# Two of eight weight loads split into one 96-row part and four 8-row parts, in an attention and swish feed-forward kernel

## The chip, the core and the metric

The kernel runs on one core of a Trainium2 chip. The metric is device time in microseconds for one execution. A profiled execution has a span, from its first to its last instruction, which is a little shorter than the device time.

The names in the text: PE does matrix products (its weight loads, PEld, run beside them), ACT applies functions and copies, DVE and POOL do elementwise work, and SP issues transfers, which are carried out by 16 DMA engines.

## The reference

Linear attention on 8 batches, 8 heads, 576 positions and a head size of 64, followed by a layer with a swish whose slope differs by channel:

```python
q_s = exp(q - max(q, -1));  q_s = q_s / sum(q_s, -1)      # softmax over the head dimension
k_s = exp(k - max(k, 2));   k_s = k_s / sum(k_s, 2)       # softmax over positions
kv  = einsum('bhsd,bhse->bhde', k_s, v)
x   = einsum('bhsd,bhde->bhse', q_s, kv)                  # then to [4608, 512]
h   = x @ w_in                                            # w_in: 512 x 2048
g   = h / (1 + exp(-beta * h))
out = g @ w_out                                           # w_out: 2048 x 512
```

Inputs and output are float32; the matrix products run in bf16.

## The kernel before

**Stages.** A chunk is 512 of a batch's 576 positions, with one batch per chunk (chunks 0 to 6 and 8); chunk 7 collects the 64 left-over positions of all eight batches. For each chunk, phase A computes 16 units of h (`unit_mm`, line 456, four matmuls of 128x512 each), a tanh on ACT (line 468) and g on DVE (line 470). Phase B (`b_mm`, line 508) multiplies g with w_out into `acc`, four tiles of 128 positions, 16 matmuls each. The matmuls of phase B are handed out in a fixed list `bq`, a few after each unit, so PE nearly always has one of the two kinds to run.

**The order is written out by hand** (`manual_schedule`, line 64): every engine runs its instructions in the order in which the program emits them.

**Start.** Batches 0 and 1 have a faster path of their own. The loads of batch 0, w_in (lines 557 to 563), beta and w_out (lines 564 and 565) are issued by SP one after the other at the program's start; those of batches 1 and 2 stand between and behind POOL's casts of w_out in the program (lines 637 to 650), but in SP's own queue they simply follow the w_out loads. Every load goes to a buffer of the pool `ld` (13 buffers), so a load also waits until the tile that had its buffer 13 loads earlier has been read.

**w_out.** The 16 slices of 128 rows come in eight loads wo0, wo2, ... wo14, each of 128 rows of 4 KB (two slices). POOL casts each to bf16 (`cast_w_out`, line 172, through the helper line 160) into `w_out_b`. The first user is phase B of chunk 0: its list takes slices 0 to 3 for the four tiles, then 4 to 7 for the four tiles, then 8 to 15 tile by tile.

**Batch 1** (`batch_1`, lines 653 to 705) follows phase A of chunk 0 in the program: 32 matmuls of phase B, then exponentials of q (`eq_exp`, line 193, ACT), their sums and divisions (`eq_sum` line 200, `eq_div` line 204, DVE), 6 and 14 more matmuls of phase B, transposes on PE (`eq_t`, line 216), exponentials of k (line 229), casts of v (line 160 on POOL, 151 on ACT, 165 on DVE), products of k and v (line 258), and x (`x_group`, line 407), with a few matmuls of phase B between them. Then phase A of chunk 1 starts.

**Completion.** In the built program, SP's transfers use eight semaphores in turn, and each transfer's issue waits until the one issued eight places before it has landed.

Of the kernel before, what the change touches and what calls it, by code (L numbers as in the profile page):

```python
# [16 lines left out]
def kernel(  # L17
# [10 lines left out]
    nc = tc.nc  # L28
    P = nc.NUM_PARTITIONS
# [38 lines left out]
    w_out_dram = moe_w_out.rearrange("(b p i) f -> b p i f", p=P, i=4)  # L68
# [23 lines left out]
    def unit(name):  # L92
        return ldp.tile([P, U], F32, tag="ld", name=name)
# [46 lines left out]

    def load_w_out(j0):
        t = unit(f"wo{j0}")[:, 0 : 2 * DM].rearrange("p (j n) -> p j n", j=2)
        nc.sync.dma_start(t, w_out_dram[j0 // 4, :, j0 % 4 : j0 % 4 + 2, :])
        ld["wo", j0] = t


# [417 lines left out]
    for j0 in range(0, NJ, 2):  # L564
        load_w_out(j0)
# [63 lines left out]
    for blk in range(1, 4):  # L629
        for k0 in (0, 2):  # L630
            if (blk, k0) == (1, 2):
                t, _ = ld["wi", 1, 2]
# [167 lines left out]
```

## Time and profile before

| What | Value |
|---|---|
| device time, three runs | 283.83, 283.87, 283.99 us (median 283.87) |
| the profiled execution | 283.87 us |
| its span | 282.1 us |
| PE busy | 274.6 us (97%), granted clock 1.0 |
| PEld, DVE, ACT, POOL busy | 135.7, 156.0, 168.4, 70.6 us |
| moved by DMA | 51.69 MB |
| w_out loads: number, size, issue to landing | 8, 512 KB, 10.3 us (median) |
| their issues by SP | 15.8 to 24.9 us from the span's start |
| POOL's casts of w_out | 8 of 1.04 us, starting at 26.1 to 35.2 us |

A reader of the profile should keep in mind that PE's busy time is counted with modelled ends, since matmuls overlap: a matmul of 128x512 counts for 379 ns but the next one starts 216 ns later. An average over the span says little here: the first 50 us have another limit than the rest, so the stages are read from timelines and windows.

The page's row of DMA activity, in 40 slices of 7.05 us, each digit the busy share in tenths, shows the same division:

```profile
DMA  7999999879699808990799059905100201031122
```

### The profile page before, as it was taken

How to read it: one execution, taken by the hardware profiler on the slowest of the kernel's cores; microseconds unless marked ns; L12 is line 12 of the kernel's file. 1: busy time of each engine (PE TensorE's matmuls, PEld its weight loads, DVE VectorE, ACT ScalarE, POOL GpSimd, SP SyncE). 2: the span in 40 equal slices, each digit the busy share in tenths (PEclk: the TensorE clock that was granted, in tenths of full speed). 3: DMA queues.
4: the chain of work that ended last, by engine and by line, in shares of the span. 5: the costliest groups of instructions: out<-in, count | busy, mean ns of one | idle time of the engine just before them, and what ended most of it. 6: DMA issues, size and time to landing. Idle time of an engine off the chain costs nothing.

```text
span 282.1 us, 4627 instructions
## 1 busy us (share of the span) xinstructions
PE 274.6 (97%) x1688; PEld 135.7 (48%) x1688; DVE 156.0 (55%) x283; ACT 168.4 (60%) x280; POOL 70.6 (25%) x116
## 2 busy tenths in 40 slices
PE   7799999999999999999999999999999999999995
PEld 3445444445444445444544444444444444444444
DVE  2768369977865475549564766476453444443301
ACT  5766368867965587557855785478454544444411
POOL 1468721550721063104510361027000000000000
PEclk9999999999999999999999999999999999999999
DMA  7999999879699808990799059905100201031122
GB/s 228 380 374 406 391 384 359 311 172 352 149 234 357 175 37 190 366 210 37 154 329 285 24 132 303 307 0 128 60 37 2 76 37 39 0 76 37 37 77 74
DMA packets 52054, 51.69 MB, mean 183 GB/s; under 512 B 21568, under 2 KB 42432, under 8 KB 52032
## 3 DMA queue, kind: packets, MB, share of 16 engines
q1 hardware_dynamic: 51888, 51.33, 60.0%
q8 instruction: 13, 0.21, 0.3%
q10 hardware_dynamic: 144, 0.07, 0.1%
q14 instruction: 9, 0.07, 0.1%
HBM read 38.28 MB, written 9.44 MB: 169 GB/s over the span
## 4 chain that ended last, share of the span: by engine, by line
PE 83%; DMA 12%; DVE 2%; ACT 0%; SPq 0%; issue 0%; ACTq 0%; POOL 0%
PE acc L508 40%; PE h L456 39%; DMA q<-in_q_dram 4%; DMA wo<-in_moe_w_out_dram 4%; DMA wi<-in_moe_w_in_dram 3%; DMA k<-in_k_dram 2%; PE kv L383 2%; PE x L407 2%; DVE Eq L204 1%; DVE qz L200 1%; ACT Eq L193 0%; SPq L116 0%; PE xt L421 0%; DVE qT L165 0%; PE kv L258 0%
## 5 line engine op out<-in xcount | busy, mean ns | idle before, releaser
L470 DVE SCALAR_TENSOR_TENSOR g<-th,h 128x512 bf16<-128x512 bf16 x144 | 97.3, 685 | 95.3 <-ACT th L468 95.0
L468 ACT ACTIVATE th<-h,beta_h 128x512 bf16<-128x512 f32 x144 | 97.2, 689 | 84.9 <-PE h L456 82.9
L508 PE MATMUL acc<-w_out_b,g 128*128 128x512 bf16 (+2 forms) x608 | 145.5, 368 | 0.0
L456 PE MATMUL h<-xT,w_in_b 128*128 128x512 bf16 x512 | 128.2, 379 | 0.0
L456 PEld LDWEIGHTS <-w_in_b 128*128 128x128 bf16 x576 | 65.0, 113 | 61.0 <-issue 0.5
L508 PEld LDWEIGHTS <-g 128*128 128x128 bf16 x608 | 56.8, 98 | 63.8 <-issue 2.5
L314 POOL TENSOR_TENSOR Eq<-Eq,qz 128x512 bf16<-128x512 bf16 x24 | 25.1, 1051 | 84.2 <-issue 41.0
L160 POOL TENSOR_SCALAR_AFFINE_SELECT va<-v 128x256 bf16<-128x256 f32 (+3 forms) x55 | 22.7, 450 | 13.8 <-DMA v<-in_v_dram 13.6
L537 ACT ACTIVATE o<-acc 128x512 f32<-128x512 f32 x34 | 20.0, 591 | 8.9 <-PE acc L508 8.9
L354 ACT ACTIVATE Ek<-k 128x640 bf16<-128x640 f32 x24 | 17.7, 736 | 0.0
L456 PE MATMUL h<-xTt,w_in_b 128*128 128x512 bf16 x64 | 16.4, 379 | 0.0
L312 DVE TENSOR_REDUCE qz<-Eq 128x8 f32<-128x512 bf16 x24 | 16.2, 676 | 0.0
L304 ACT ACTIVATE Eq<-q 128x512 bf16<-128x512 f32 x24 | 14.7, 622 | 0.0
L200 DVE TENSOR_REDUCE qz<-Eq 128x16 f32<-128x1024 bf16 x4 | 4.9, 1214 | 10.4 <-ACT Eq L193 10.4
L165 DVE CAST xT<-x 128x512 bf16<-128x512 f32 x15 | 10.3, 684 | 0.6 <-PE x L407 0.6
L581 PE MATMUL warm<-zf 128*128 128x512 f32 (+1 forms) x14 | 8.8, 772 | 1.5 <-DVE zf L548 1.5
L151 ACT CAST xT<-x 128x512 bf16<-128x512 f32 x17 | 9.7, 578 | 0.6 <-PE x L407 0.5
L160 POOL TENSOR_SCALAR_AFFINE_SELECT w_in_b<-wi 128x512 bf16<-128x512 f32 x15 | 9.2, 633 | 3.3 <-DMA wi<-in_moe_w_in_dram 3.1
L193 ACT ACTIVATE Eq<-q 128x1024 bf16<-128x1024 f32 x4 | 4.2, 1057 | 9.0 <-DMA q<-in_q_dram 9.0
L340 POOL TENSOR_TENSOR Et<-Et,zt 128x512 bf16<-128x512 bf16 x4 | 4.2, 1042 | 20.9 <-DVE zt L339 15.6
L160 POOL TENSOR_SCALAR_AFFINE_SELECT w_out_b<-wo 128x1024 bf16<-128x1024 f32 x8 | 8.3, 1042 | 1.8 <-DMA wo<-in_moe_w_out_dram 1.7
L407 PE MATMUL x<-qT,kvn 64*64 64x512 bf16 x64 | 5.8, 391 | 0.8 <-ACT xT L151 0.6
(48 smaller groups left out, 76.5 us busy)
## 6 DMA issues: line engine op xcount, KB each, us to landing
q<-in_q_dram SPq DMA_DIRECT2D x16, 512.0 KB, 6.0
out_dram<-o SPq DMA_DIRECT2D x31, 256.0 KB, 3.1
k<-in_k_dram SPq DMA_DIRECT2D x24, 320.0 KB, 6.6
v<-in_v_dram SPq DMA_DIRECT2D x24, 320.0 KB, 7.3
wo<-in_moe_w_out_dram SPq DMA_DIRECT2D x8, 512.0 KB, 10.3
wi<-in_moe_w_in_dram SPq DMA_DIRECT2D x6, 512.0 KB, 8.0
k<-in_k_dram SPq DMA_DIRECT2D x4, 576.0 KB, 9.1
v<-in_v_dram SPq DMA_DIRECT2D x6, 288.0 KB, 8.9
```

The lines of the kernel that those rows point to most:

```text
L160: nc.gpsimd.affine_select(out=dst, in_=src, pattern=[[0, n]], base=0, channel_multiplier=0, compare_op=ALU.is_equal, fill=fill0,)
L165: eng.tensor_copy(dst, src)
L304: nc.scalar.activation(by_pair(Eq[b], m).rearrange("p t h d -> p h t d"), ld["q", b, hf][:, a : a + 2, :].rearrange("p h (t d) -> p h t d" ...
L312: nc.vector.tensor_reduce(z, e, axis=AX.X, op=ALU.add)
L314: nc.gpsimd.tensor_tensor(e, e, z.unsqueeze(3).to_broadcast((P, NT, 2, D)), ALU.mult)
L354: nc.scalar.activation(Ek[b][:, :, h0:h1, :].rearrange("p t h d -> p h t d"), ld["k", b, hf][:, a : a + h1 - h0, :].rearrange("p h (t d) - ...
L407: nc.tensor.matmul(xps[b, 2 * g + c][o, :], kvn[b][r, j, :], qT[b][r, g, a] if b < EARLY else qT[b][r, :, j, :], start=True, stop=True,)
L456: nc.tensor.matmul(hs[n, i][:], w_in_b[:, kt, blk * CH + r : (blk + 1) * CH : 4], rhs_a(n, kt), start=(kt == 0), stop=(kt == KT - 1),)
L468: nc.scalar.activation(th[:], h[:], ACTF.Tanh, scale=beta_h[:, i // 4, i % 4 : i % 4 + 1])
L470: nc.vector.scalar_tensor_tensor(out=g[:], in0=th[:], scalar=1.0, in1=h[:], op0=ALU.add, op1=ALU.mult)
L508: nc.tensor.matmul(acc[n, st][:, c0:c1], gs[n, j][:, min(st, 3) * P : (min(st, 3) + 1) * P], w_out_b[:, j, c0:c1], start=(j == 0), stop=(j ...
L537: nc.scalar.activation(o[:], acc[n, st][:], ACTF.Copy, scale=0.5)
```

## The change

Two of the eight w_out loads, wo4 and wo10, are no longer one transfer of 128 rows. Their first 96 rows are one transfer; the other 32 rows are four transfers of 8 rows each, which are meant to run as one row on each of the first eight DMA engines. All five are issued by SP, one after the other, at the place of the old load. The tile, the bytes and the rest of the program stay the same; SP has 8 transfers more. The beta load behind w_in's second block stands in both kernels.

```diff
     def load_w_out(j0):
         t = unit(f"wo{j0}")[:, 0 : 2 * DM].rearrange("p (j n) -> p j n", j=2)
-        nc.sync.dma_start(t, w_out_dram[j0 // 4, :, j0 % 4 : j0 % 4 + 2, :])
+        src = w_out_dram[j0 // 4, :, j0 % 4 : j0 % 4 + 2, :]
+        if j0 in (4, 10):
+
+            nc.sync.dma_start(t[0:96], src[0:96])
+            for r in range(96, P, 8):
+                nc.sync.dma_start(t[r : r + 8], src[r : r + 8])
+        else:
+            nc.sync.dma_start(t, src)
         ld["wo", j0] = t
```

## The prediction

> **What bounds the kernel now.** I read the page's chain of waits first, then the timelines of the engines around its DMA part, then a table of windows. In the chain, the listing of its longest pieces in order of time (start, duration, what) has only DMA until 36.63 us and hardly anything but PE later:
>
> ```profile
> 15.77 10.30 DMA wo<-in_moe_w_out_dram
> 26.15 10.46 DMA q<-in_q_dram
> 36.63 1.06 ACT Eq L193
> 37.72 1.23 DVE qz L200
> 39.26 1.22 DVE Eq L204
> 40.48 1.14 DVE qz L200
> 41.94 1.23 DVE Eq L204
> ```
>
> Read it downward: a w_out load, the first q load of batch 1 (q1_0), its exponential on ACT, and four steps of DVE with only reciprocals between them. The DMA engines are the bound of the first 50 us, and the point at which their lateness becomes PE's is batch 1. The windows (length, busy time of PE, PEld, DVE, ACT, POOL with instructions, granted clock, DMA share, GB/s) show it, and one late stage that I need below:
>
> ```profile
> 28.00:32.00 4.00, 4.00 (x20) 1.92 (x19) 2.61 (x5) 2.42 (x4) 3.28 (x4) 1.00 1.03 410
> 40.00:44.00 4.00, 3.90 (x46) 2.22 (x44) 3.89 (x9) 3.63 (x8) 1.70 (x3) 1.00 1.07 374
> 44.00:48.00 4.00, 3.85 (x37) 1.61 (x35) 3.44 (x9) 3.03 (x8) 0.46 (x2) 1.00 1.08 358
> ...
> 248.06:249.30 1.24, 1.24 (x7) 0.60 (x6) 0.69 (x1) 0.21 (x1) 0.00 (x0) 1.00 0.97 207
> ```
>
> DMA share is 1 or above while w_out comes in, at 410 GB/s. PE is covered (4.00 of 4.00) and loses only 0.10 + 0.15 us between 40 and 48. How little slack is left there is read from PE's timeline (start, duration):
>
> ```profile
> 29.48 11.39 PE L508 MATMUL acc<-w_out_b,g 128*128 128x512 bf16 x52
> 40.70 0.61 PE L216 MATMUL tp<-ident,Eq 128*128 128x128 bf16 x8
> ...
> 42.52 0.60 PE L508 MATMUL acc<-w_out_b,g 128*128 128x512 bf16 x2
> 43.22 0.62 PE L216 MATMUL tp<-ident,Eq 128*128 128x128 bf16 x8
> ```
>
> The first division (line 204) ends at 39.26 + 1.22 = 40.48 and PE's transposes of it begin at 40.70: 0.22 us of slack. The second ends at 41.94 + 1.23 = 43.17, and PE starts 0.05 us later: none. So what delays q1_0 by D beyond 0.2 us delays PE by D once both transposes are through, and PE has no hole afterwards in which to recover it.
>
> **How the loads flow.** POOL's casts of w_out (line 160) start as each load lands:
>
> ```profile
> 27.41 1.04 POOL L160 TENSOR_SCALAR_AFFINE_SELECT w_out_b<-wo 128x1024 bf16<-128x1024 f32 x1 [0.23 <-DMA wo<-in_moe_w_out_dram]
> 28.68 1.04 POOL L160 TENSOR_SCALAR_AFFINE_SELECT w_out_b<-wo 128x1024 bf16<-128x1024 f32 x1 [0.23 <-DMA wo<-in_moe_w_out_dram]
> 29.97 1.04 POOL L160 TENSOR_SCALAR_AFFINE_SELECT w_out_b<-wo 128x1024 bf16<-128x1024 f32 x1 [0.25 <-DMA wo<-in_moe_w_out_dram]
> ```
>
> A load of 512 KB per 1.28 us. With 128 rows on 16 engines that is 8 rows each, 0.16 us per 4 KB row. From issue to landing it takes 10.3 us, so some eight loads stand in the queue. The trace also keeps 16 completion marks for every transfer, without the engine's number: for q1_0 the first stands at 34.77, the ninth at 35.31, the last at 36.61. This spread of 1.84 us is almost the same for all w_out loads (28.14, 28.71, 29.91 for wo6): some engines run behind for the whole stage, and only the last one releases the consumer.
>
> **The change, part by part.**
>
> *Other engines.* The built programs have the same instructions in the same order on PE, DVE, ACT and POOL; SP gets 8 more issues (4 after wo4, 4 after wo10). POOL's casts of these two tiles wait for five transfers in place of one.
>
> *The 96-row part.* 6 rows per engine by 0.16 = 0.96 us in place of 1.28. If rows 0 to 95 don't spread as evenly as 128 it may cost the old 1.28. I take 0.96.
>
> *The single-row loads.* Eight rows on eight engines, four times per tile. Free running, each costs those engines 0.16 us. From the other side: the nearest row of a transfer that touches few partitions is the stage of 64-partition stores, where at a DMA share of 0.97 the rate is 207 GB/s, half of 410. In proportion to partitions, 8 of them would get 26 GB/s, and 32 KB would take 1.27 us. So 0.16 to 1.27 us each. The row has only one halving in it, and I take that: 0.32 us. Per tile the eight engines then spend 0.96 + 4 x 0.32 = 2.24 us in place of 1.28, +0.96; for two tiles +1.92. The bounds: 0.96 + 4 x 0.16 = 1.60, +0.32 per tile, +0.64 for both; and 1.28 + 4 x 1.27 = 6.36, +5.1 per tile, +10.2 for both. The eight other engines are spared 2 rows per tile, 0.64 us for both.
>
> [...]
>
> *Who is late.* Which eight engines are meant can't be seen in the marks. If the last engine is among them, the landing is late by the full +1.92. If the latest of them is only the second last (1.53 behind the first, where the last is 1.83), by 1.92 - 0.30 = 1.6. One of these two holds in 3 of 4 draws of 8 out of 16. I take 1.8.
>
> *SP.* In the built program every load waits for the one issued eight places before it. The small loads fill places, so q1_0, which waited for wo0 and issued at 26.15, now waits for wo8, landing at 31.19 before, and is issued 5 us later. Its first packets are wanted at about 33.3, the first mark of wo14 before it; the first load of the kernel was issued at 0.80 and its packets started at 1.93, so they can start at 31.2 + 1.1 = 32.3. Covered by 1.0 us. The four small loads of wo10 wait for wo4's parts (28.6), and SP's issues of loads take 0.33 to 0.85 us, so wo12 is issued at 30.3 to 32.3 in place of 23.51, and starts at 31.4 to 33.4; the last engine reaches it at 32.5. That is 0 to 0.9 us; I take 0, and keep 0.9 for the range. Behind these issues in SP's queue stand wo12, wo14, q1, k1, v1 and batch 2. As 8 issues were added, each load from q2 on waits for the same one as before.
>
> *w_out itself.* A late cast would stop PE only beyond its slack. wo10's cast ends at 33.57; PE takes its rows as matmuls 35 and 36 of the 52 that start at 29.48, at 36.9: 3.3 us. wo14's ends at 36.20 and is wanted at 37.8: 1.6 us. A lateness of 1.8 just reaches the latter (0.2 us), and this is part of the same 1.8, not beside it: the transposes wait for q1_0 anyway.
>
> **Sum.** 1.8 us on q1_0, less 0.22 at the first transposes, and the 0.22 returns at the second ones, where PE already waits: +1.8 us. The profiled execution took 283.87 us (282.1 of span and 1.8 around it), as the median of the runs does. 283.87 + 1.8 = 285.7.
>
> **The rivals.**
>
> *A, the eight engines lead.* Should these be the early ones and rows cost 0.16, then the late ones are spared 0.64 us and everything from q1_0 on lands 0.64 earlier. PE can use it: it idles 0.25 us by the windows, and by its starts the matmuls at 43.22, 44.63 and 44.96 come 0.26, 0.22 and 0.24 later than where PE doesn't wait, 0.72 in all. 283.87 - 0.64 = 283.2. For it: the spread exists, and 0.64 is near the gap between its halves (the second eight of the marks begin 0.57 after the first). Against it: the very last engine, 0.7 behind the next at wo6, must be spared too, and the rows must be free of the halving.
>
> *B, the eight engines hold the last one, and rows run freely.* +0.64: 284.5. For it: DMA share of 1 through the stage. Against: needs the few partitions to cost nothing.
>
> *C, it cancels.* Early engines take the extra within their 1.5 us of lead, the last one isn't touched, or is spared what SP's late issue takes back: 283.9. The point from which this gives way is a lateness of 0.2 us at q1_0.
>
> **How the numbers follow.** Forecast 0.55 (285.7; its own range 284.6 to 288), B 0.16 (284.5), A 0.16 (283.2), C 0.13 (283.9). About 0.2% (0.57 us) can be told from no change: all of the forecast and most of B are slower, 0.70; most of A faster, 0.15; the rest 0.15. The range reaches down to A, 283.2, and up to 288.0: that is a second halving, 0.64 us per small load, 0.96 + 2.56 = 3.52 and +2.24 per tile, +4.5 for both, less the 0.3 of the second-last engine. The proportional bound, +10.2, lies beyond; I leave it, SP's 0.9 on top of a high case and the edge below A to the 2 in 10.
>
> **What would show it.** The landing of q1_0, thus the start of line 193's exponential at 36.63: at 38.4 by the forecast, 37.3 by B, 36.0 by A. The third and sixth casts of w_out start late, with idle time ended by wo. PE's idle time between 37 and 48 grows from 0.25 to about 2 us by the forecast, and there is no other new hole up to the end. DMA share falls below 1 between 27 and 34, as the spared engines run dry. I would be wrong if the small loads land 0.16 us apart; or if the stop were at the casts and q1_0 on time.

## The result

| | Before | After |
|---|---|---|
| median of four runs | 283.93 us | 288.10 us |
| lowest to highest | 283.83 to 284.38 | 287.82 to 289.15 |
| the profiled execution | 283.87 us, span 282.1 | 287.82 us, span 286.1 |
| PE busy | 274.6 us | 275.1 us |
| q1_0 landed (its last mark) | 36.61 us | 40.10 us |

The change costs 4.2 us: the ratio is 1.0151, with an interval of 1.0123 to 1.0178. The direction was foreseen. The size was not: 285.7 was forecast, with a range up to 288.0.

In the changed kernel's code the lines from 143 on stand 7 lower: the cast helper is line 167 (was 160), `eq_exp` 200 (was 193), `eq_t` 223 (was 216), phase B 515 (was 508). Line 146 issues the 96-row parts, 148 the 8-row loads and 150 the whole loads.

First the windows of the changed kernel (start:end; length; busy time of PE, PEld, DVE, ACT and POOL with instructions; granted clock; DMA share; GB/s):

```profile
24.00:28.00 4.00, 4.00 (x20) 2.11 (x19) 3.01 (x6) 2.42 (x4) 2.51 (x5) 1.00 1.00 288
28.00:32.00 4.00, 3.31 (x17) 1.52 (x15) 2.71 (x5) 2.42 (x4) 2.67 (x3) 1.00 0.89 283
32.00:36.00 4.00, 4.00 (x20) 1.80 (x19) 0.00 (x0) 0.00 (x0) 2.65 (x4) 1.00 0.80 210
36.00:40.00 4.00, 3.43 (x16) 1.46 (x15) 0.00 (x0) 0.00 (x0) 2.96 (x3) 1.00 0.99 355
40.00:44.00 4.00, 2.54 (x12) 0.98 (x10) 2.72 (x4) 2.67 (x3) 0.00 (x0) 1.00 1.04 388
```

Before, the first and the third of these windows read (the second stands in the prediction, with 410 GB/s at 1.03):

```profile
24.00:28.00 4.00, 4.00 (x21) 2.06 (x19) 3.16 (x7) 2.42 (x4) 3.51 (x6) 1.00 1.03 409
32.00:36.00 4.00, 4.00 (x21) 1.81 (x19) 0.00 (x0) 0.00 (x0) 3.21 (x4) 1.00 1.06 369
```

Read the last two columns together. In the first window the share is still 1.00, so the 16 engines are busy nearly all the time (0.90 between 26.5 and 27.5 us), and yet they move 288 in place of 409 GB/s: each 4 KB packet takes longer. In the trace the packets of 4 KB that start between 26 and 28 us take 159 to 171 ns before; in the changed kernel nine in ten of them take 211 to 488 ns. In the second and third window the share falls as well, to 0.89 and 0.80: there the queue also runs dry for part of the time.

POOL's timeline shows the loads landing one by one, and what its casts waited for:

```profile
28.16 1.05 POOL L167 TENSOR_SCALAR_AFFINE_SELECT w_out_b<-wo 128x1024 bf16<-128x1024 f32 x1 [1.22 <-DMA wo<-in_moe_w_out_dram]
29.77 1.04 POOL L167 TENSOR_SCALAR_AFFINE_SELECT w_out_b<-wo 128x1024 bf16<-128x1024 f32 x1 [0.56 <-DMA wo<-in_moe_w_out_dram]
31.42 1.04 POOL L167 TENSOR_SCALAR_AFFINE_SELECT w_out_b<-wo 128x1024 bf16<-128x1024 f32 x1 [0.61 <-DMA wo<-in_moe_w_out_dram]
32.88 1.04 POOL L167 TENSOR_SCALAR_AFFINE_SELECT w_out_b<-wo 128x1024 bf16<-128x1024 f32 x1 [0.42 <-DMA wo<-in_moe_w_out_dram]
34.85 3.17 POOL L167 TENSOR_SCALAR_AFFINE_SELECT w_out_b<-wo 128x1024 bf16<-128x1024 f32 x3 [0.93 <-DMA wo<-in_moe_w_out_dram]
38.26 1.04 POOL L167 TENSOR_SCALAR_AFFINE_SELECT w_out_b<-wo 128x1024 bf16<-128x1024 f32 x1 [0.25 <-DMA wo<-in_moe_w_out_dram]
```

These are wo0, wo2, wo4, wo6, then wo8, wo10 and wo12 in one line, then wo14. Even wo0, which was issued ahead of the split loads and is itself unchanged, is 2.0 us late (its last mark is at 28.10, before at 26.07). 0.9 us of this is older than the split rows: the last mark of w_in's last load, ahead of wo0 in the queue, is already at 25.70, before at 24.79, and the w_in loads ahead of that one are 0.8 us late by their last marks. The other 1.1 us fall into the time in which the other engines turn to wo4: the other 15 marks of wo2 end at 26.64, and those of wo4's 96 rows begin at 26.91, ahead of wo0's last at 28.10. How much of the 4.2 us comes from the early lag isn't shown. It isn't the cause of the price: in experiments 2, 3 and 9 below, which lose as much or more, the same mark of w_in is at 24.85, 24.70 and 24.91.

Then PE's timeline, and ACT's exponential of q1_0:

```profile
30.86 7.93 PE L515 MATMUL acc<-w_out_b,g 128*128 128x512 bf16 x36 [0.69 <-POOL w_out_b L167]
39.36 3.18 PE L515 MATMUL acc<-w_out_b,g 128*128 128x512 bf16 x14 [0.57 <-POOL w_out_b L167]
44.12 0.61 PE L223 MATMUL tp<-ident,Eq 128*128 128x128 bf16 x8 [1.58 <-DVE Eq L211]
```

```profile
40.12 1.06 ACT L200 ACTIVATE Eq<-q 128x1024 bf16<-128x1024 f32 x1 [9.22 <-DMA q<-in_q_dram]
```

The exponential starts 3.49 us later than before (36.63). PE stops three times. By the starts of neighbouring matmuls, less the usual 216 ns, the holes are 0.85, 0.73 and 1.75 us: twice for a cast of w_out, once for the division of q1_0. The products of k and v of the next batch are 3.83 us later than before (64.00 against 60.18). One more hole stands at 67.08, where x waits 0.42 us for a transpose by DMA (line 414); by the starts it is 0.49 longer than before. From 82 us on PE runs 4.3 us behind to its last matmul; the tail after that is 0.3 us shorter, so that the span grows by 4.0.

The chain of waits in order of time (start, duration, what) shows where SP comes into it:

```profile
17.71 13.60 DMA wo<-in_moe_w_out_dram
31.31 0.02 issue
31.32 0.29 SPq L148
...
32.73 4.19 DMA wo<-in_moe_w_out_dram
36.91 0.06 issue
36.97 0.81 POOL w_out_b L167
```

The 8-row loads of wo10 wait for wo4's 96-row part, which lands at 31.31. Behind them in SP's queue, wo12 is issued at 32.73, where it was at 23.51, and lands 4.2 us later. The same happens earlier to wo6: it stands behind wo4's small loads and is issued at 25.76, where it was at 18.73.

### The profile page after: what moved, and what is told of

It is laid out like the page before. It is cut to its first block, busy times and chain, and to the rows that moved or that the text cites. A ratio compares the mean times of both kernels' runs of the same rounds, so it can differ in the third digit from the quotient of the medians.

```text
span 286.1 us, 4639 instructions
## 1 busy us (share of the span) xinstructions
PE 275.1 (96%) x1688; PEld 135.5 (47%) x1688; DVE 156.0 (55%) x283; ACT 168.4 (59%) x280; POOL 70.4 (25%) x116
## 4 chain that ended last, share of the span: by engine, by line
PE 75%; DMA 21%; SPq 1%; issue 1%; POOL 1%; ACT 0%; POOLq 0%; ACTq 0%
PE acc L515 38%; PE h L463 35%; DMA wo<-in_moe_w_out_dram 6%; DMA v<-in_v_dram 6%; DMA k<-in_k_dram 3%; DMA wi<-in_moe_w_in_dram 3%; DMA qT<-Eq 2%; DMA out_dram<-o 2%; PE kv L390 1%; PE x L414 1%; SPq L148 0%; SPq L116 0%; POOL w_out_b L167 0%; PE xt L428 0%; SPq L104 0%
## 6 DMA issues: line engine op xcount, KB each, us to landing
v<-in_v_dram SPq DMA_DIRECT2D x6, 288.0 KB, 9.2
```

## The experiments

Two theories stood first. **Shape:** the rows of a split load don't spread over the partitions as 128 do, and the engines are slow while they run. **Places:** the eight added transfers fill the eight places of SP's semaphores, so that later loads are issued too late. All times are medians; every ratio is against the kernel before, run in the same set on the same chip (283.95 to 284.04 us). The edits are shown against the changed kernel, unless another is named; three dots stand for lines left out.

### 1. Eight tiny loads without a split

wo4 and wo10 stay whole; behind each come four loads of 8 rows by 64 bytes into a tile that nothing reads.

```diff
+    tiny = const.tile([P, 16], F32, name="tiny")
...
         if j0 in (4, 10):
...
-            nc.sync.dma_start(t[0:96], src[0:96])
+            nc.sync.dma_start(t, src)
             for r in range(96, P, 8):
-                nc.sync.dma_start(t[r : r + 8], src[r : r + 8])
+                nc.sync.dma_start(tiny[r : r + 8], w_out_dram[0, r : r + 8, 0, 0:16])
```

> wo4 and wo10 are whole 128-row loads again; behind each stand four loads of 8 rows of 64 bytes into a tile that nobody reads. So the eight additional issues and their places in the queue are kept, and the split of the tile is gone. Theory 'conflict' (rows of the pieces land on partitions that other engines are writing, so packets take longer): 283.8 to 284.4 us, and q1_0's exponential at 36.5 to 37.0. Theory 'places' (SP waits for the transfer eight places before, so wo12, wo14 and q1 are issued late and the queue runs dry): most of the 4.2 us stays, 286.5 to 288, wo12 issued at 30 us or later.

Measured: 286.75 us, ratio 1.0089 [1.0060, 1.0119]; q1_0 landed at 39.68. Eight places cost 2.5 us with next to no bytes in them. Its windows:

```profile
24.00:28.00 4.00, 3.95 (x19) 2.08 (x19) 3.94 (x8) 2.77 (x5) 3.41 (x6) 1.00 1.01 372
28.00:32.00 4.00, 4.00 (x20) 1.94 (x19) 2.89 (x5) 2.42 (x4) 3.10 (x3) 1.00 0.82 270
32.00:36.00 4.00, 4.00 (x20) 1.76 (x19) 0.00 (x0) 0.00 (x0) 2.08 (x2) 1.00 0.94 258
```

Here it is mainly the share that falls (0.82): most 4 KB packets still take 159 to 162 ns, but for part of the time there are none. So places are a cause by themselves. Whether they are the cause in the changed kernel is another question, since its first window is slow at a nearly full share.

### 2. Small loads of every fourth row

```diff
-            for r in range(96, P, 8):
-                nc.sync.dma_start(t[r : r + 8], src[r : r + 8])
+            for r in range(4):
+                nc.sync.dma_start(t[96 + r : P : 4], src[96 + r : P : 4])
```

> As the changed kernel, but each of the 8-row loads takes every fourth row from 96 on, in place of eight neighbours. Same bytes, same number of transfers, same 96-row part. Theory 'neighbours' (the eight rows of a small load get in each other's way because they are neighbours): 285 to 286.5. Theory 'places': 288, unchanged. Theory '96 rows' (the 96-row part and its uneven split is what slows the engines): 287 to 288.

Measured: 288.34 us, 1.0146 [1.0128, 1.0164]. Taking every fourth row in place of eight neighbours gains nothing; q1_0 lands at 40.91, not earlier than in the changed kernel. So the price isn't that eight neighbouring partitions are slow in a small load. The profile of this run has one disturbance of its own, told in the last section; it doesn't make the price, since two other executions, with a granted clock of 1.0, took 288.38 and 288.44 us.

### 3. One load of 32 rows in place of four of 8

```diff
             nc.sync.dma_start(t[0:96], src[0:96])
-            for r in range(96, P, 8):
-                nc.sync.dma_start(t[r : r + 8], src[r : r + 8])
+            nc.sync.dma_start(t[96:P], src[96:P])
```

> The tile still comes as 96 rows and 32 rows, but the 32 rows are one transfer on all engines in place of four, so 2 additional issues in place of 8. Theory 'neighbours': 284 to 285. Theory 'places': 284 to 285. Theory '96 rows': 286 to 287.5.

Measured: 288.34 us, 1.0154 [1.0131, 1.0176]: the whole price of the change, with two transfers more in place of eight, and above the 287.5 that the shape theory had allowed for. The windows, from the fastest of its runs (287.23 us):

```profile
24.00:28.00 4.00, 3.95 (x19) 2.12 (x19) 3.12 (x6) 2.53 (x5) 2.81 (x5) 1.00 1.05 307
28.00:32.00 4.00, 3.94 (x19) 1.73 (x18) 2.48 (x4) 2.32 (x4) 2.16 (x3) 1.00 1.03 311
32.00:36.00 4.00, 4.00 (x20) 1.86 (x19) 0.00 (x0) 0.00 (x0) 2.00 (x2) 1.00 1.01 290
```

The share is above 1 in all three, so the queue doesn't run dry, and the rate is 290 to 311 GB/s in place of 369 to 410. Of the packets of 4 KB that start between 26 and 28 us, nine in ten take 246 to 313 ns. The split into 96 and 32 rows makes the engines slow, the earliest too: wo6's first mark is at 29.52, before at 28.14. Which of the two parts does it isn't shown, since no run has one without the other.

### 4. Only wo4 split

```diff
-        if j0 in (4, 10):
+        if j0 in (4,):
```

> Only wo4 is split as in the changed kernel; wo10 is whole. If the two splits cost alike, about 286. If the second one, whose small loads are issued only when wo4 has landed, is what empties the queue ('places'): 284.5 to 285.3. If the first one alone already slows all engines and wo10 adds little ('conflict'): 286 to 287.5.

Measured: 286.21 us, 1.0078 [1.0051, 1.0105]: half of the change, so the second tile adds about as much as the first.

### 5 and 6. Splits that reach every part of the partitions

The same bytes in two transfers per tile, once by columns (128 rows of 2 KB each), once by even and odd rows (64 rows of 4 KB each).

```diff
         if j0 in (4, 10):
-            nc.sync.dma_start(t[0:96], src[0:96])
...
+            for j in range(2):
+                nc.sync.dma_start(t[:, j], src[:, j])
```

> [...] Theory '96 rows' (with other row counts the engines write partitions that another engine is writing, and packets take 260 to 310 ns in place of 160): the cost is gone, 283.9 to 284.6 us, DMA at 400 GB/s in 24 to 32 us. Theory 'any split costs' (two more transfers and their places are what costs): 286 to 288.

```diff
         if j0 in (4, 10):
-            nc.sync.dma_start(t[0:96], src[0:96])
...
+            for r in range(2):
+                nc.sync.dma_start(t[r:P:2], src[r:P:2])
```

> wo4 and wo10 are split into even and odd rows: two transfers of 64 rows each, whose rows reach over all partitions, as the later k and v loads of the kernel do. Theory '96 rows' in the form that coverage of the partitions decides: 283.9 to 285. In the form that only the 128-row order keeps engines apart: 286 to 288.5, with DMA at 300 GB/s or less between 24 and 32 us at a share near 1.

Measured: columns 284.33 us, 1.0016 [1.0007, 1.0026]; even and odd rows 284.15 us, 1.0010 [1.0001, 1.0019]. The windows of the latter:

```profile
24.00:28.00 4.00, 3.95 (x19) 2.13 (x19) 3.24 (x7) 2.67 (x5) 3.52 (x6) 1.00 1.03 410
28.00:32.00 4.00, 4.00 (x21) 1.88 (x19) 2.95 (x5) 2.42 (x4) 3.28 (x4) 1.00 1.03 410
32.00:36.00 4.00, 4.00 (x20) 1.83 (x19) 0.00 (x0) 0.00 (x0) 3.24 (x4) 1.00 1.06 370
```

These are the rates of before, with as many transfers as in experiment 3. Two transfers in place of one are not the price.

### 9. The same two transfers, as lower and upper half

The edit is against experiment 6.

```diff
-            for r in range(2):
-                nc.sync.dma_start(t[r:P:2], src[r:P:2])
+            for r in (0, 64):
+                nc.sync.dma_start(t[r : r + 64], src[r : r + 64])
```

> wo4 and wo10 are split into rows 0 to 63 and rows 64 to 127: two transfers of 64 rows, as with even and odd rows (which took 284.15 us, +0.15), but each covers one half of the partitions. Theory 'coverage' (what costs is that 16 engines share the partitions of a half, or the uneven 96): 285.5 to 288.5, packets slowed, DMA at 310 GB/s or less between 24 and 32 us at a share near 1. If 96 is costly as a number of rows alone (6 rows per engine): 283.9 to 284.6.

Measured: 289.38 us, 1.0194 [1.0178, 1.0209]: slower than the change itself, and above what the shape theory had allowed for.

```profile
24.00:28.00 4.00, 3.95 (x19) 2.12 (x19) 3.33 (x6) 2.42 (x4) 3.02 (x5) 1.00 1.05 280
28.00:32.00 4.00, 3.49 (x17) 1.55 (x16) 2.48 (x4) 2.42 (x4) 1.42 (x2) 1.00 1.04 295
32.00:36.00 4.00, 3.10 (x15) 1.36 (x14) 0.00 (x0) 0.00 (x0) 2.10 (x3) 1.00 1.02 239
```

Experiments 6 and 9 have the same number of transfers, of rows and of bytes, and rows of 4 KB in both; only which 64 rows go together differs. The one runs at 410, 410 and 370 GB/s, the other at 280, 295 and 239 with a share above 1. Of the 4 KB packets that start between 26 and 28 us, nine in ten take 159 to 168 ns in the one and 268 to 452 ns in the other. This is the pair that settles the cause, as far as this: which rows go together.

Why the one runs at 410 GB/s in the first window and the other at 280 isn't shown: with the partition of the tile, the row read from DRAM changes too in every run here, and no run separates the two.

### 7, 10, 11 and 12. How many places, and where

Tiny loads as in experiment 1, fewer of them: one behind each of the two loads, both into the same rows of the scratch tile (7); four behind wo4 alone (10); four behind wo10 alone (11); one behind each, into different rows (12). The scratch tile is read by nothing. The edits of 7, 10 and 11 are against experiment 1, that of 12 against 7.

```diff
             nc.sync.dma_start(t, src)
-            for r in range(96, P, 8):
-                nc.sync.dma_start(tiny[r : r + 8], w_out_dram[0, r : r + 8, 0, 0:16])
+            nc.sync.dma_start(tiny[0:8], w_out_dram[0, 0:8, 0, 0:16])
```

> wo4 and wo10 are whole; behind each stands one tiny load (8 rows of 64 bytes) in place of four (which took 286.8 us, +2.7). Theory 'places' with a margin (the queue holds about ten us of work and runs dry only if several places go to small transfers): 283.8 to 284.4. If each place costs alike: 2 of 8, +0.7, 284.6 to 284.8.

```diff
-        if j0 in (4, 10):
+        if j0 == 4:
```

> All loads whole; four tiny loads behind wo4 only (eight tiny loads behind wo4 and wo10: 286.8, +2.7). Theory 'places' with a margin: the queue's ten us cover four places, 283.9 to 284.6. Each place costing alike: +1.35, 285.3.

```diff
-        if j0 in (4, 10):
+        if j0 == 10:
```

> All loads whole; four tiny loads behind wo10 only. Theory 'places' with a margin: 283.9 to 284.6, wo12 issued at 28.7 us in place of 30.5. Each place costing alike: 285.3. If the place close ahead of q1 is what matters: 286 and more.

```diff
-            nc.sync.dma_start(tiny[0:8], w_out_dram[0, 0:8, 0, 0:16])
+            r = 8 * j0
+            nc.sync.dma_start(tiny[r : r + 8], w_out_dram[0, r : r + 8, 0, 0:16])
```

> One tiny load behind wo4 and one behind wo10, as in the run before of that kind (284.55 us), but into different rows of the scratch tile: there the second wrote the rows of the first, so SP held it until 29.2 us. Theory 'places' with a margin: 283.8 to 284.2, with the second tiny load issued at 24.8. If each place costs by itself: 284.5 again.

| Tiny loads | Median | Ratio | Loss by the ratio | Per load |
|---|---|---|---|---|
| 8 (experiment 1) | 286.75 us | 1.0089 [1.0060, 1.0119] | 2.5 us | 0.32 us |
| 4 behind wo4 (10) | 285.36 us | 1.0050 [1.0035, 1.0065] | 1.4 us | 0.36 us |
| 4 behind wo10 (11) | 285.01 us | 1.0044 [1.0031, 1.0058] | 1.2 us | 0.31 us |
| 1 and 1, other rows (12) | 284.59 us | 1.0024 [1.0014, 1.0034] | 0.7 us | 0.34 us |
| 1 and 1, same rows (7) | 284.55 us | 1.0019 [1.0010, 1.0028] | 0.5 us | 0.27 us |

I had expected a margin: the first few places free, and a price only once the queue runs dry. The medians show none: two loads already cost 0.5 to 0.7 us. In experiment 7 the second tiny load also has to wait for the first one's landing, because it writes the same rows (SP held it until 29.2 us); experiment 12 takes that wait away, and the time stays (284.59 against 284.55 us). With four tiny loads the queue is seen dry: the share is 0.89 between 28 and 32 us in experiment 10 and 0.86 between 32 and 36 us in experiment 11. With two into the same rows the share is 0.96 between 28 and 32 us, at 351 GB/s (experiment 7). With two into different rows it doesn't fall:

```profile
24.00:28.00 4.00, 3.95 (x19) 2.07 (x19) 3.56 (x7) 2.54 (x5) 3.52 (x6) 1.00 1.03 410
28.00:32.00 4.00, 4.00 (x20) 1.94 (x19) 2.67 (x5) 2.42 (x4) 3.28 (x4) 1.00 1.03 410
32.00:36.00 4.00, 4.00 (x20) 1.77 (x19) 0.00 (x0) 0.00 (x0) 3.13 (x4) 1.00 1.06 366
```

This is experiment 12, with the rates of before, and q1_0 still lands 0.5 us late (37.12). The marks show that this lateness is older than the tiny loads. The last mark of w_in's last load is at 25.24, before at 24.79, and at 25.09 in experiment 7. That is 0.45 and 0.30 us of the 0.51 and 0.33 us by which q1_0 is late in these two executions, and w_in's loads that landed before the first tiny load was even issued lag already. So the two traces put next to nothing on the added places, and the margin isn't refuted. Over all fourteen traces this mark lies between 24.59 and 25.70; one trace of each kernel can't say whether the lag belongs to the kernel or to the execution. What makes the 0.5 to 0.7 us of the medians is open.

### 8. A remedy tried: q1_0 ahead of the last w_out load

In the kernel before, without any split, q1_0 is issued in front of wo14.

```diff
+        if j0 == 14:
+            load_q(1, 0)
...
-            for hf in range(2):
-                load_q(1, hf)
+            load_q(1, 1)
```

> The kernel before, with the first q load of batch 1 issued ahead of wo14 in place of behind it; nothing is split. q1_0 should land 1.3 us earlier, at 35.3, and wo14 1.5 later, at 36.6; its cast then ends at 37.7, just when PE wants it (37.8). If DVE's chain from q1_0 is what PE waits for at 43.2 and 44.6 us: 283.2 to 283.7. If wo14's cast comes too late: 283.9 to 284.5.

Measured: 283.85 us, 0.9999 [0.9990, 1.0008]: no difference. In the profiled execution q1_0 lands at 35.67, 0.94 us earlier, but wo14's cast is late in its stead, and PE stops there:

```profile
38.12 3.18 PE L508 MATMUL acc<-w_out_b,g 128*128 128x512 bf16 x14 [0.53 <-POOL w_out_b L160]
```

The hole has moved from the transposes to the matmuls ahead of them. This execution took 284.23 us, 0.38 above the median, and the last mark of w_in's last load was 0.47 us later than before (25.26), so the hole may be smaller in the others. None of the kernels tried beats the one before.

## Why the prediction was wrong in its size

**Right: the way from DMA to PE.** The forecast was that the DMA engines bound the first 50 us, that q1_0's lateness beyond 0.2 us becomes PE's, and that PE has nothing with which to recover. q1_0 was 3.49 us late, batch 2's products 3.83 us, and the last matmul 4.3 us. Two details were off. PE also stopped for two casts of w_out: for wo14's (0.73 us), whose slack I had expected to be reached only just, and for wo2's (0.85 us), which I had left out. These two holes are no loss on top: PE passes them while it would otherwise wait for q1_0, and its hole there is 1.75 in place of some 3.3 us. And "no other new hole" was wrong by the 0.49 us at 67.

**Right: the price of a small load.** I took 0.32 us. In the trace wo4's four loads finish 0.26 to 0.39 us after one another. The loss that the forecast missed lay elsewhere.

**The step that failed: the 96-row part, and the engines beside it.** I took 0.96 us for the part ("6 rows per engine by 0.16") and at most the old 1.28, and wrote that "the eight other engines are spared 2 rows per tile". By the ninth of the 16 marks, wo4's 96 rows follow wo2 by 1.56 us (26.01 to 27.57). So the part costs 0.6 us more than I took, and 0.28 more than my upper bound, while the small loads come on top as forecast. No gain for the others is seen either. The last engine isn't among the eight (their marks of wo4's small loads end at 29.20, while its mark of the 96 rows ahead of them is only at 31.31), and these 6 rows took it 1.60 us, where 8 rows took 1.27 before. My mistake was to count rows per engine at a fixed 0.16 us. I read the 207 GB/s of the half-partition stores and used it for the small loads alone, though 96 of 128 partitions are a part too. Experiment 3 shows that the 96 and 32 rows alone make the whole loss, and 6 against 9 that it is which rows go together that matters.

**Mis-sized: SP.** I took 0 for the late issues, with 0.9 as the bound. wo12 was expected to be issued between 30.3 and 32.3 and was at 32.73, and it landed 4.2 us after that. I had left out wo6, which was issued 7 us late, at 25.76. Experiment 1 puts a price on the eight places where nothing else is changed: 2.5 us. In the changed kernel this doesn't come on top: experiment 3 has two added places and loses as much as the change with eight. The runs show that the two prices don't add up; that a slow queue lasts longer and so hides late issues is my reading of it, and isn't shown. The early lag of 0.9 us in the profiled execution is a third term that the prediction doesn't have; what it adds isn't shown.

**The rivals.** A, that the eight engines lead and the late ones gain 0.64 us, fell in an instructive way. The marks of the 8-row loads don't include the last engine, so the laggard was indeed among those to be spared, as A needed. It was slowed with the rest all the same: in the changed kernel the last engine stands 2.7 to 2.9 us behind the first at w_in's last four loads and 4.4 at wo4, where it was 1.8 throughout before. B (284.5) and C (283.9) fell with the slow packets.

**The signs.** The exponential of q1_0 was forecast at 38.4 and came at 40.12. The late casts came, but from the first one on (wo0), not from the third. The fall of the DMA share between 27 and 34 came (0.89, then 0.80). I read it as the late issues: wo6 was only issued at 25.76, just ahead of the first fall, and experiment 1 falls to 0.82 with no engine spared a row. The trace doesn't name the engines that ran dry.

## What to carry to other kernels

Split a 128-row load so that each piece still reaches across all partitions: here the splits by columns (284.33 us, a ratio of 1.0016) and by every second row (284.15, 1.0010) cost little, while those into contiguous parts took 288.34 (96 + 32 rows, 1.0154) and 289.38 (64 + 64, 1.0194). The contiguous parts slowed what ran beside them too, loads issued ahead of them included: wo2 landed at 28.50 in experiment 3 and at 29.16 in experiment 9, before at 27.35. Where loads stand in a full queue and a fixed number of them may be outstanding (eight in this program), count each added transfer, however small: here eight cost 2.5 us and four 1.2 to 1.4. Read DMA share and GB/s together: 280 GB/s at a share of 1.05 were slow packets (268 to 452 ns, experiment 9), 270 GB/s at 0.82 a queue that was dry for part of the time, with most packets at 159 to 162 ns (experiment 1).

## What was not expected of the hardware

**One engine runs behind, and instruction fetches may be why.** Of the 16 marks of a load, the last came 1.8 us after the first all through the stage in the kernel before. It falls behind between the w_in loads that land at 18.67 and 20.73 (from the first mark to the last 1.05 us, then 1.76). At 18.1 us the trace has a packet of 16 KB for instructions that takes 1.1 us; the profile's page lists these under queue q8. In the changed kernel the packet is at 18.26, and the distance from the first mark to the last grows from 1.2 to 2.7 us there. This is a coincidence in time, and no run moved the fetch.

**The granted clock fell after two holes.** In experiment 2, PE waited twice in a row for a cast, and the window that begins there has a granted clock of 0.57; the 14 matmuls there took 4.87 us, where 14 take 3.18 in the changed kernel:

```profile
40.00:44.00 4.00, 3.78 (x10) 1.41 (x10) 1.91 (x3) 2.20 (x3) 0.17 (x1) 0.57 1.06 391
```

```profile
38.91 0.38 PE L514 MATMUL acc<-w_out_b,g 128*128 128x512 bf16 x1 [1.40 <-POOL w_out_b L166]
40.22 4.87 PE L514 MATMUL acc<-w_out_b,g 128*128 128x512 bf16 x14 [0.93 <-POOL w_out_b L166]
```

By the starts, less 216 ns, the first hole is 1.57 us. Each cast of w_out releases two matmuls, but the trace has one record between the holes, 51 in place of the 52 up to the transposes. With a second one put at 39.13, 216 ns behind the first, the second hole is 0.88 us, by this estimate. In the changed kernel three holes of 0.85, 0.73 and 1.75 us lie 8 and 5 us apart, and the clock stays at 1.00 in every window shown. It stays at 1.00 in experiment 9 too, with holes of 0.73, 0.56 and, by the same estimate, 0.85 us that end at 39.01, 40.00 and 41.29. No run varied the holes alone.
